# Linear attention block: how x arrives transposed, which queue carries the other loads, and where the q tiles stand

## The chip, the cores and the metric

The kernel runs on one core of a Trainium2 chip. The metric is the time of one execution on the device in microseconds, the median of several runs. "TensorE", "VectorE", "ScalarE", "GpSimd" and "SyncE" appear in the profile as PE (with PEld for its weight loads), DVE, ACT, POOL and SP. "SPq" and "ACTq" are the DMA-issuing instructions of SP and ACT.

## The reference

One linear attention block on x of shape 1 x 2048 x 640 with 32 heads of 20 columns, in bf16:

```python
qkv = x @ wqkv                      # 640 -> 3 * 640, split in q, k, v per head
phi = lambda t: where(t > 0, t + 1, exp(t)) + 1e-6
pq, pk = phi(q), phi(k)
kv  = einsum("bhsd,bhse->bhde", pk, v)      # 20 x 20 per head
z   = einsum("bhsd->bhd", pk)
num = einsum("bhqd,bhde->bhqe", pq, kv)
den = einsum("bhqd,bhd->bhq", pq, z)[..., None] + 1e-6
out = (num / den) @ wo
```

## The kernel before, in words

x is needed in two layouts: as it stands (`xn`, rows on the partitions) and transposed (`xT`, columns on the partitions). Transposed blocks are written by DMA transposes, `load_xT` (line 167): x is cut into five blocks of rows (`XCH`, line 162: 256, 256, 512, 512, 512 rows), and each block into five column tiles of 128, which gives 25 transposes, all issued by SP.

The work has four stages.

1. **k stage**, `k_tile` (line 220), 16 tiles of 128 rows. For each half of the columns TensorE does five matmuls of 128x320 (line 225) with a block of `xT` as weights and `wk` moving; ACT takes the exponential (L235), DVE does the minimum (L237) and the sum that gives `pk` (L240). Eight PSUM banks hold four tiles.
2. **state stage**, `p_step` (line 245): for each half of the columns and each of the 16 row tiles five matmuls (L249) add x-transposed times pk into banks 0 to 4. In each half two q tiles (`q_tile`, line 269: five matmuls of 128x512, then ACT and DVE as in the k stage; L275, L283, L285, L288) stand between the steps and two behind them, in banks 5 to 7. There are 20 q tiles in all. DVE adds up z (L294).
3. **middle**: z is finished (`z_finish`), the state is multiplied with wv (`kv_group`), masked, and multiplied with wo (`w2_group`, six groups). The resulting matrix w2 goes out to DRAM and back in another row order (`w2_rows`: a write of two DMAs, a wait, five reads). The rest of the q tiles, the denominators (`den`: matmuls L391, two ACT operations) and the division (`normalize`, L407) stand between.
4. **output stage**, `out_tile` (line 410), 16 tiles: ten matmuls (L416), copies by ACT and DVE, a DMA out.

Before the k stage TensorE does `warm(n)` matmuls of 128x512 on zeros (L216).

The order on each engine is the order of the calls in the program's text. A small planner (`Plan`, line 18) adds the semaphore waits: an operation waits until the writers of what it reads, and the readers and writers of what it writes, are done; a PSUM bank is such a thing. Each engine runs its list strictly in order, and an engine that issues a DMA (SP, or ACT between its operations) can do nothing else until that issue is through. `w_cols` loads the columns of wqkv; `load_rest` (line 184) issues, all on ACT: `wk` in two halves, `wqn`, the four quarters of `xn`, `wv`, `wog` in two pieces, and then the load of ACT's function table. `permute_wq` (line 205) reorders `wqn` into `wqp` on POOL, which the q tiles read.

Of the kernel before, what the change touches and what calls it, by code (L numbers as in the profile page):

```python
# [82 lines left out]
def bass_standalone__linear_attn_block__prompt_kernel(nc, x, wqkv, wo, out):  # L83
    B, S, D = x.shape
    assert (B, S, D) == (1, 2048, 640)
    H, DH = 32, 20
    NC_ = D // 128
    NT = S // 128
    HALF = D // 2
# [5 lines left out]
    with contextlib.ExitStack() as ctx:  # L95
# [48 lines left out]
        def pool_const():  # L144
            P.add("dve", lambda e: e.memset(zero[:, :], 0.0), writes=["zero"])
            P.add("dve", lambda e: e.memset(ones[:, :], 1.0), writes=["ones"])
            P.add("dve", lambda e: e.memset(eps[:, :], 1e-6), writes=["eps"])  # L147
            P.add("pool", lambda e: e.memset(wv[:, NC_ * D:], 0.0), writes=["wvpad"])
            P.add("pool", lambda e: e.memset(hm[:, :], 1.0), writes=["hm"])
            P.add("pool", lambda e: e.memset(bm[:, :], 1.0), writes=["bm"])  # L150
            for t, w, name in ((hm, 4, "hm"), (bm, DH, "bm")):
                n = t.shape[1] // w
                for lo in (True, False):
                    P.add("pool", lambda e, t=t, w=w, n=n, lo=lo: e.affine_select(
                        out=t[:, :].rearrange("p (a b) -> p a b", b=w),
                        in_=t[:, :].rearrange("p (a b) -> p a b", b=w),
                        pattern=[[-w if lo else w, n], [0, w]],
                        base=0 if lo else w - 1,
                        channel_multiplier=1 if lo else -1,
                        compare_op=ALU.is_ge, fill=0.0), reads=[name], writes=[name])  # L160
# [5 lines left out]

        def load_xT():
            for i, (a, b) in enumerate(XCH):
                for c in range(NC_):
                    P.add("sp", lambda e, a=a, b=b, c=c: e.dma_start(  # L170
                        xT[:, c * S + a:c * S + b], x[0, a:b, 128 * c:128 * c + 128],
                        transpose=True), writes=[("xT", i, c)], dma=True)

        def xT_keys(a, b):
            return [("xT", i, c) for i, (p, q) in enumerate(XCH) if p < b and a < q
                    for c in range(NC_)]

        def w_cols(dst, lo, hi, col, key, eng="act"):
            P.add(eng, lambda e: e.dma_start(
                dst[:, 0:NC_ * D].rearrange("p (c n) -> p c n", n=D)[:, :, lo:hi],  # L180
                wqkv[:, col + lo:col + hi].rearrange("(c p) n -> p c n", p=128)),
                writes=[key], dma=True)

        def load_rest():
            w_cols(wk, 0, HALF, D, ("wk", 0))
            w_cols(wk, HALF, D, D, ("wk", 1))
            w_cols(wqn, 0, D, 0, "wqn")
            for q in range(4):
                P.add("act", lambda e, q=q: e.dma_start(
                    xn[:, 4 * q * D:4 * (q + 1) * D].rearrange("p (t n) -> p t n", n=D),  # L190
                    x[0, 512 * q:512 * (q + 1), :].rearrange("(t p) n -> p t n", p=128)),
                    writes=[("xn", q)], dma=True)
            w_cols(wv, 0, D, 2 * D, "wv")
            P.add("act", lambda e: e.dma_start(
                wog[0:GW, 0:5 * D].rearrange("p (g n) -> p g n", n=D),
                wo[0:5 * GW, :].rearrange("(g p) n -> p g n", p=GW)),
                writes=["wog"], dma=True)
            P.add("act", lambda e: e.dma_start(
                wog[0:gsz[5], 5 * D:6 * D], wo[5 * GW:D, :]), writes=["wog5"], dma=True)
            tl = mybir.InstLoadActFuncSet(  # L200
                name=nc.get_next_instruction_name(),
                act_func_set_id=ACT_TABLE_SET_LN_EXP, ins=[], outs=[])
            P.add("act", lambda e: e.add_instruction(tl), writes=["table"])  # L203

        def permute_wq():

# [7 lines left out]
        def warm(n):  # L214
            for _ in range(n):
                P.add("pe", lambda e: e.matmul(  # L216
                    bank(7), zero[:, 0:128], zero[:, :], start=True, stop=True),
                    reads=["zero"], writes=[("bank", 7)])
# [103 lines left out]
        def z_finish(b):  # L322
            def mm(e):
                for c in range(NC_):
                    r = e.matmul(bank(b, 1, off=c), zs[:, 128 * c:128 * c + 128],
                                 ones[:, 0:1], start=True, stop=True)
                return r
            P.add("pe", mm, reads=["zs", "ones"], writes=[("bank", b)])
            P.add("dve", lambda e: e.tensor_copy(zc[:, 0:NC_], bank(b, NC_)),
                  reads=[("bank", b)], writes=["zc"])  # L330
            for c in range(NC_):
                P.add("dve", lambda e, c=c: e.tensor_scalar(  # L332
                    zb[:, 128 * c:128 * c + 128], hm[:, :], zc[:, c:c + 1], None, ALU.mult),
                    reads=["hm", "zc"], writes=[("zb", c)])
# [27 lines left out]
        def w2_group(g, b):  # L362
            n = gsz[g]
            for h in range(2):
                P.add("pe", lambda e, h=h: e.matmul(
                    bank(b + h, HALF, parts=n), kvt[0:n, GW * g:GW * g + n],
                    wog[0:n, g * D + HALF * h:g * D + HALF * (h + 1)], start=True, stop=True),
                    reads=[("kvt", 0 if g < 4 else g - 3), "wog", "wog5"],
                    writes=[("bank", b + h)])
            P.add("act", lambda e: e.copy(  # L370
                fold(w2g[0:n, g * D:(g + 1) * D]), two_banks(b, parts=n)),
                reads=[("bank", b), ("bank", b + 1)], writes=[("w2g", g)])
# [15 lines left out]
        def den(sbk, b):  # L388
            def mm(e):
                for c in range(NC_):  # L390
                    r = e.matmul(bank(b), zb[:, 128 * c:128 * c + 128],  # L391
                                 pq[:, c * S + BK * sbk:c * S + BK * (sbk + 1)],
                                 start=(c == 0), stop=(c == NC_ - 1))
                return r
            P.add("pe", mm, reads=[("zb", c) for c in range(NC_)]
                  + [("pq", sbk, c) for c in range(NC_)], writes=[("bank", b)])
            i = sbk % 2
            P.add("act", lambda e: e.activation(lb[i][:, :], bank(b), ACTF.Ln, bias=eps[:, 0:1]),  # L398
                  reads=[("bank", b), "eps", "table"], writes=[("lb", i)])
            P.add("act", lambda e: e.activation(rd[i][:, :], lb[i][:, :], ACTF.Exp, scale=-1.0),  # L400
                  reads=[("lb", i)], writes=[("rd", i)])

        def normalize(sbk):
            i = sbk % 2
            for c in range(NC_):
                v = pq[:, c * S + BK * sbk:c * S + BK * (sbk + 1)]
                P.add("dve", lambda e, v=v: e.tensor_tensor(v, v, rd[i][:, :], ALU.mult),  # L407
                      reads=[("rd", i), ("pq", sbk, c)], writes=[("pq", sbk, c)])
# [20 lines left out]
                reads=[("osb", j, 0), ("osb", j, 1)], writes=[("out", st)], dma=True)  # L429


        pool_const()
        load_xT()
        load_rest()
        permute_wq()
        warm(9)
        for st in range(NT):
            k_tile(st)
        zst = z_steps()
# [3 lines left out]
        def next_q(b):  # L443
            q_tile(*qs[qi[0]], b)
            qi[0] += 1

        for h in range(2):
            for st in range(NT):
                p_step(h, st)
                if zst and st % 2 == 1:  # L450
                    zst.pop(0)()
                if st in (5, 11):
                    next_q(5 + qi[0] % 3)
            p_out(h)
            next_q(5 + qi[0] % 3)
            next_q(5 + qi[0] % 3)
        for f in zst:
            f()
        z_finish(4)

        kv_group(0)
        next_q(5)
        next_q(6)
        den(0, 7)
        w2_group(0, 2)
        w2_group(1, 0)
        normalize(0)
        next_q(5)
        w2_group(2, 2)
        w2_group(3, 0)  # L470
        next_q(6)
        den(1, 7)
        w2_group(4, 2)
        w2_group(5, 0)
        w2_rows()
        normalize(1)
        while qi[0] < 15:
            next_q((3, 4, 5, 6)[qi[0] % 4])
        next_q(3)
        next_q(4)  # L480
        den(2, 7)
        next_q(5)
        normalize(2)
        next_q(6)
        next_q(2)
        for st in range(2):
            out_tile(st)
        den(3, 6)
# [56 lines left out]
```

## Time and profile before

| | us |
|---|---|
| median of 3 runs (131.49 to 131.9) | 131.84 |
| the profiled execution | 131.94 |
| its span, first to last instruction | 130.2 |
| TensorE busy (share of the span) | 105.9 (81%) |
| VectorE busy | 66.6 (51%) |
| ScalarE busy | 41.9 (32%) |
| first k matmul starts | 14.92 |
| first state matmul starts | 48.78 |
| first output matmul starts | 103.74 |

All times of the trace count from the start of the span. The profiled execution lies 1.7 us above its span. A row of the timeline gives the start, the time taken, the engine, the line and the operation, merged over equal neighbours, and in brackets the idle time before it with what ended it. In the view of waits, a row reads: who waited, for whom, microseconds in all, how often, the longest. Queue q1 carries what SP issues, q10 what ACT issues; in the views of the DMA, a queue's row gives packets, megabytes and the share of 16 engines.

### The profile page before, as it was taken

The numbers are of one execution on the slowest core, as the hardware profiler recorded it, in microseconds if no ns is written. First come the engines' busy times: TensorE is split into PE (matmuls) and PEld (weight loads), VectorE is DVE, ScalarE is ACT, GpSimd is POOL, SyncE is SP. The second block draws the span as 40 slices with busy tenths as digits, with TensorE's granted clock in tenths as the row PEclk, the third lists the DMA queues.
The fourth block names the chain that finished last, engine by engine and source line by source line (L and its number), as shares of the span: only waits on it lengthen the run. The fifth ranks groups of instructions, "written<-read, shape, count | busy, mean of one in ns | idle before, by whom it ended". The sixth has DMA issues, their size and how long they took to land.

```text
span 130.2 us, 1712 instructions
## 1 busy us (share of the span) xinstructions
PE 105.9 (81%) x655; PEld 65.1 (50%) x661; DVE 66.6 (51%) x132; ACT 41.9 (32%) x73; POOL 5.7 (4%) x16
## 2 busy tenths in 40 slices
PE   6600498309999979999999999989599689999991
PEld 2100254105677757666566668534244256777770
DVE  0000015700488889899923056767586963743431
ACT  0000062301255450101601034288756425323230
POOL 7009000000000000000000000000000000000000
PEclk9999999975799999999999999999999999999999
DMA  3999999994553000000000000000273511243332
GB/s 76 316 249 278 339 321 301 210 198 89 118 58 70 0 0 0 5 0 3 3 0 0 5 0 0 0 0 0 59 196 91 162 44 57 103 151 104 137 114 101
DMA packets 20137, 12.88 MB, mean 99 GB/s; under 512 B 11554, under 2 KB 20130, under 8 KB 20130
## 3 DMA queue, kind: packets, MB, share of 16 engines
q1 hardware_dynamic: 14729, 6.89, 22.4%
q10 hardware_dynamic: 5401, 5.90, 16.1%
q8 instruction: 5, 0.08, 0.3%
q14 instruction: 2, 0.02, 0.0%
HBM read 6.72 MB, written 3.44 MB: 78 GB/s over the span
## 4 chain that ended last, share of the span: by engine, by line
PE 63%; SPq 15%; DVE 6%; ACT 6%; DMA 6%; issue 2%
PE ps L249 17%; PE ps L416 16%; SPq L170 15%; PE ps L225 14%; PE ps L275 13%; DMA xT<-in_x_dram 6%; PE ps L391 3%; DVE pq L288 2%; ACT lb L398 2%; ACT w2g L370 1%; DVE pq L407 1%; ACT rd L400 1%; ACT eq L283 1%; DVE eq L285 1%; DVE zb L332 1%
## 5 line engine op out<-in xcount | busy, mean ns | idle before, releaser
L225 PE MATMUL ps<-wk,xT 128*128 128x320 bf16 x160 | 27.3, 341 | 15.5 <-DMA xT<-in_x_dram 15.0
L225 PEld LDWEIGHTS ps<-wk,xT 128*128 128x128 bf16 x160 | 17.3, 110 | 26.1 <-issue 17.3
L275 PE MATMUL ps<-xT,wqp 128*128 128x512 bf16 x95 | 22.5, 379 | 1.7 <-ACT w2g L370 1.4
L416 PE MATMUL ps<-w2p,pq 128*128 128x320 bf16 x160 | 22.2, 299 | 1.8 <-DMA w2p<-w_rows 1.2
L249 PE MATMUL ps<-pk,xn 128*128 128x320 bf16 x160 | 22.7, 299 | 0.7 <-DVE pk L240 0.7
L283 ACT ACTIVATE eq<-ps 128x512 bf16<-128x512 f32 x20 | 11.9, 597 | 27.2 <-PE ps L275 26.7
L237 DVE TENSOR_SCALAR ek<-ek 128x640 bf16<-128x640 bf16 x16 | 5.2, 327 | 29.9 <-ACT ek L235 29.9
L416 PEld LDWEIGHTS ps<-w2p,pq 128*128 128x128 bf16 x160 | 15.5, 98 | 8.6 <-issue 1.7
L249 PEld LDWEIGHTS ps<-pk,xn 128*128 128x128 bf16 x160 | 15.5, 98 | 8.0 <-DVE pk L240 1.0
L235 ACT ACTIVATE ek<-ps 128x640 bf16<-128x640 f32 x16 | 11.3, 704 | 19.4 <-PE ps L225 19.3
L275 PEld LDWEIGHTS ps<-xT,wqp 128*128 128x128 bf16 x100 | 9.6, 98 | 11.7 <-ACT w2g L370 1.7
L288 DVE SCALAR_TENSOR_TENSOR pq<-ps,eq 128x512 bf16<-128x512 f32 x20 | 13.8, 692 | 0.7
L240 DVE SCALAR_TENSOR_TENSOR pk<-ps,ek 128x640 bf16<-128x640 f32 x16 | 13.2, 825 | 0.5
L425 DVE CAST osb<-ps 128x320 bf16<-128x320 f32 x16 | 7.8, 490 | 10.8 <-PE ps L416 10.8
L285 DVE TENSOR_SCALAR eq<-eq 128x512 bf16<-128x512 bf16 x20 | 5.8, 292 | 13.5 <-ACT eq L283 13.2
L423 ACT CAST osb<-ps 128x320 bf16<-128x320 f32 x16 | 6.8, 425 | 14.7 <-PE ps L416 14.7
L407 DVE TENSOR_TENSOR pq<-pq,rd 128x512 bf16<-128x512 bf16 x20 | 7.1, 420 | 3.8 <-ACT rd L400 3.8
L203 ACT ACT_TABLE_LOAD x1 | 1.3, 1283 | 16.9 <-issue 16.9
L294 DVE TENSOR_TENSOR za<-pk 128x1280 f32<-128x1280 bf16 x4 | 5.8, 1482 | 0.0
L216 PE MATMUL ps<-zero 128*128 128x512 bf16 x9 | 4.0, 631 | 1.3 <-DVE eps L147 1.3
L391 PE MATMUL ps<-pq,zb 128*128 128x512 bf16 x19 | 4.8, 379 | 0.1
L294 DVE TENSOR_TENSOR za<-za 128x1280 f32<-128x1280 f32 x3 | 4.4, 1483 | 0.0
(30 smaller groups left out, 35.0 us busy)
## 6 DMA issues: line engine op xcount, KB each, us to landing
xn<-in_x_dram ACTq DMA_DIRECT2D x4, 640.0 KB, 12.6
out_dram<-osb SPq DMA_DIRECT2D x16, 160.0 KB, 1.8
wk<-in_wqkv_dram ACTq DMA_DIRECT2D x2, 400.0 KB, 4.2
wqn<-in_wqkv_dram ACTq DMA_DIRECT2D x1, 800.0 KB, 8.0
wv<-in_wqkv_dram ACTq DMA_DIRECT2D x1, 800.0 KB, 14.9
w2p<-w_rows SPq DMA_DIRECT2D x5, 160.0 KB, 2.8
wog<-in_wo_dram ACTq DMA_DIRECT2D x1, 750.0 KB, 17.5
w_rows<-w2g SPq DMA_DIRECT2D x1, 750.0 KB, 5.3
```

The costliest lines, as they stand in the source:

```text
L170: P.add("sp", lambda e, a=a, b=b, c=c: e.dma_start(xT[:, c * S + a:c * S + b], x[0, a:b, 128 * c:128 * c + 128], transpose=True), writes=[ ...
L225: r = e.matmul(bank(b + h, HALF), xT[:, c * S + 128 * st:c * S + 128 * st + 128], wk[:, c * D + HALF * h:c * D + HALF * (h + 1)], start=(c ...
L235: P.add("act", lambda e: e.activation(fold(t[:, :]), two_banks(b), ACTF.Exp), reads=banks + ["table"], writes=[("ek", st % 3)])
L240: P.add("dve", lambda e: e.scalar_tensor_tensor(fold(pk[:, st * D:(st + 1) * D]), two_banks(b), 0.0, fold(t[:, :]), ALU.max, ALU.add), rea ...
L249: r = e.matmul(bank(d, HALF), xn[:, st * D + 128 * d:st * D + 128 * d + 128], pk[:, st * D + HALF * h:st * D + HALF * (h + 1)], start=(st ...
L275: r = e.matmul(bank(b), wqp[:, d * D + 128 * c:d * D + 128 * c + 128], xT[:, d * S + BK * sbk:d * S + BK * (sbk + 1)], start=(d == 0), sto ...
L283: P.add("act", lambda e: e.activation(t[:, :], bank(b), ACTF.Exp), reads=[("bank", b), "table"], writes=[("eq", i)])
L288: P.add("dve", lambda e: e.scalar_tensor_tensor(pq[:, c * S + BK * sbk:c * S + BK * (sbk + 1)], bank(b), 0.0, t[:, :], ALU.max, ALU.add), ...
L294: P.add("dve", lambda e: e.tensor_tensor(d_ap, a, b, ALU.add), reads=ra + rb, writes=[dst])
L391: r = e.matmul(bank(b), zb[:, 128 * c:128 * c + 128], pq[:, c * S + BK * sbk:c * S + BK * (sbk + 1)], start=(c == 0), stop=(c == NC_ - 1))
L407: P.add("dve", lambda e, v=v: e.tensor_tensor(v, v, rd[i][:, :], ALU.mult), reads=[("rd", i), ("pq", sbk, c)], writes=[("pq", sbk, c)])
L416: r = e.matmul(bank(b + h, HALF), pq[:, c * S + 128 * st:c * S + 128 * st + 128], w2p[:, c * D + HALF * h:c * D + HALF * (h + 1)], start=( ...
```

## The change

Each block of rows of x is transposed by one DMA transpose over all 640 columns, so that five instructions stand in place of 25, and `xT` has one key per block in place of five. `wk` stays on ACT, with the table load right behind it; `wqn`, `xn`, `wv` and `wog` are issued by SP, behind the five transposes. The warm-up has 16 matmuls in place of 9. In each half of the state stage one q tile is taken out; the middle gets two more, and its order is another: the w2 groups stand singly between q tiles, `z_finish` comes behind the first of them, and the denominators use bank 4 in place of 7.

```diff
         def load_xT():
             for i, (a, b) in enumerate(XCH):
-                for c in range(NC_):
-                    P.add("sp", lambda e, a=a, b=b, c=c: e.dma_start(
-                        xT[:, c * S + a:c * S + b], x[0, a:b, 128 * c:128 * c + 128],
-                        transpose=True), writes=[("xT", i, c)], dma=True)
+                P.add("sp", lambda e, a=a, b=b: e.dma_start_transpose(
+                    xT[:, :].rearrange("p (c s) -> p c s", s=S)[:, :, a:b], x[0, a:b, :]),
+                    writes=[("xT", i)], dma=True)
...
-        def load_rest():
-            w_cols(wk, 0, HALF, D, ("wk", 0))
-            w_cols(wk, HALF, D, D, ("wk", 1))
-            w_cols(wqn, 0, D, 0, "wqn")
...
+        def load_wk():
+            w_cols(wk, 0, HALF, D, ("wk", 0), "act")
+            w_cols(wk, HALF, D, D, ("wk", 1), "act")
...
+        def load_rest():
+            w_cols(wqn, 0, D, 0, "wqn", "sp")
+            for q in range(4):
+                P.add("sp", lambda e, q=q: e.dma_start(
...
+        load_wk()
+        load_xT()
         pool_const()
-        load_xT()
         load_rest()
         permute_wq()
-        warm(9)
+        warm(16)
...
-                if st in (5, 11):
+                if st == 7:
                     next_q(5 + qi[0] % 3)
...
-        z_finish(4)
-
         kv_group(0)
         next_q(5)
+        z_finish(4)
+        w2_group(0, 2)
         next_q(6)
-        den(0, 7)
-        w2_group(0, 2)
         w2_group(1, 0)
+        den(0, 4)
+        next_q(7)
+        w2_group(2, 2)
+        next_q(5)
+        w2_group(3, 0)
         normalize(0)
+        next_q(6)
+        w2_group(4, 2)
+        next_q(7)
+        w2_group(5, 0)
+        den(1, 4)
+        w2_rows()
         next_q(5)
-        w2_group(2, 2)
-        w2_group(3, 0)
         next_q(6)
-        den(1, 7)
-        w2_group(4, 2)
-        w2_group(5, 0)
-        w2_rows()
         normalize(1)
         while qi[0] < 15:
-            next_q((3, 4, 5, 6)[qi[0] % 4])
+            next_q((7, 2, 3, 5, 6)[qi[0] % 5])
+        next_q(0)
+        next_q(1)
+        den(2, 4)
+        next_q(2)
+        normalize(2)
         next_q(3)
-        next_q(4)
-        den(2, 7)
         next_q(5)
-        normalize(2)
-        next_q(6)
-        next_q(2)
         for st in range(2):
             out_tile(st)
```

On SP, at the program's start, before and then with the change (the tile that is written, the DRAM tensor that is read, the shape, the count):

```order
L170 DMA_TRANSPOSE xT<-in_x_dram 128x256 x10
L170 DMA_TRANSPOSE xT<-in_x_dram 128x512 x15
L375 DMA w_rows<-w2g 120x5x640
L379 DMA w_rows<-w2g 40x640
L383 DMA w2p<-w_rows 128x1x640 x5
```

```order
L169 DMA_TRANSPOSE xT<-in_x_dram 128x5x256 x2
L169 DMA_TRANSPOSE xT<-in_x_dram 128x5x512 x3
L177 DMA wqn<-in_wqkv_dram 128x5x640
L193 DMA xn<-in_x_dram 128x4x640 x4
L177 DMA wv<-in_wqkv_dram 128x5x640
L198 DMA wog<-in_wo_dram 120x5x640
L202 DMA wog<-in_wo_dram 40x640
L375 DMA w_rows<-w2g 120x5x640
```

The 25 transposes have become five, and the eight loads that ACT issued now stand between them and the write of w2.

On ACT, at the program's start, the difference between the two (minus is before):

```order
-L179 DMA wk<-in_wqkv_dram 128x5x320 x2
-L179 DMA wqn<-in_wqkv_dram 128x5x640
-L189 DMA xn<-in_x_dram 128x4x640 x4
-L179 DMA wv<-in_wqkv_dram 128x5x640
-L194 DMA wog<-in_wo_dram 120x5x640
-L198 DMA wog<-in_wo_dram 40x640
-L203 ACT_TABLE_LOAD
+L177 DMA wk<-in_wqkv_dram 128x5x320 x2
+L188 ACT_TABLE_LOAD
```

Eight DMA issues have left the place ahead of the table load and the first exponential.

On PE, from the multiplication with wv (L344) to the output (L416), as it stands with the change (L325 is z, L365 w2, L275 a q tile of five matmuls, L391 a denominator):

```order
L344 MATMUL ps<-pt,wv 40x40 x5
L275 MATMUL ps<-xT,wqp 128x512 x5
L325 MATMUL ps<-ones,zs 128x1 x5
L365 MATMUL ps<-wog,kvt 120x320 x2
L275 MATMUL ps<-xT,wqp 128x512 x5
L365 MATMUL ps<-wog,kvt 120x320 x2
L391 MATMUL ps<-pq,zb 128x512 x5
...
L365 MATMUL ps<-wog,kvt 40x320 x2
L391 MATMUL ps<-pq,zb 128x512 x5
L275 MATMUL ps<-xT,wqp 128x512 x25
L391 MATMUL ps<-pq,zb 128x512 x5
L275 MATMUL ps<-xT,wqp 128x512 x15
```

Before, the w2 matmuls stood in runs of four; now each pair has a q tile or a denominator between it and the next. Behind the last pair there are one denominator, five q tiles, one denominator and three q tiles ahead of the output, as there were before without the first denominator.

More of the change, by code (lines that the diff above doesn't have):

```diff
@@ L168, in load_xT, with w_cols @@
             for i, (a, b) in enumerate(XCH):
-                for c in range(NC_):
-                    P.add("sp", lambda e, a=a, b=b, c=c: e.dma_start(
-                        xT[:, c * S + a:c * S + b], x[0, a:b, 128 * c:128 * c + 128],
-                        transpose=True), writes=[("xT", i, c)], dma=True)
+                P.add("sp", lambda e, a=a, b=b: e.dma_start_transpose(
+                    xT[:, :].rearrange("p (c s) -> p c s", s=S)[:, :, a:b], x[0, a:b, :]),
+                    writes=[("xT", i)], dma=True)
         def xT_keys(a, b):
-            return [("xT", i, c) for i, (p, q) in enumerate(XCH) if p < b and a < q
-                    for c in range(NC_)]
-        def w_cols(dst, lo, hi, col, key, eng="act"):
+            return [("xT", i) for i, (p, q) in enumerate(XCH) if p < b and a < q]
+        def w_cols(dst, lo, hi, col, key, eng):
             P.add(eng, lambda e: e.dma_start(
@@ L182, in w_cols @@
                 writes=[key], dma=True)
-        def load_rest():
-            w_cols(wk, 0, HALF, D, ("wk", 0))
-            w_cols(wk, HALF, D, D, ("wk", 1))
-            w_cols(wqn, 0, D, 0, "wqn")
[L188 to L199, printed above, removed]
+        def load_wk():
+            w_cols(wk, 0, HALF, D, ("wk", 0), "act")
+            w_cols(wk, HALF, D, D, ("wk", 1), "act")
             tl = mybir.InstLoadActFuncSet(
@@ L203, in load_rest @@
             P.add("act", lambda e: e.add_instruction(tl), writes=["table"])
+        def load_rest():
+            w_cols(wqn, 0, D, 0, "wqn", "sp")
+            for q in range(4):
+                P.add("sp", lambda e, q=q: e.dma_start(
+                    xn[:, 4 * q * D:4 * (q + 1) * D].rearrange("p (t n) -> p t n", n=D),
+                    x[0, 512 * q:512 * (q + 1), :].rearrange("(t p) n -> p t n", p=128)),
+                    writes=[("xn", q)], dma=True)
+            w_cols(wv, 0, D, 2 * D, "wv", "sp")
+            P.add("sp", lambda e: e.dma_start(
+                wog[0:GW, 0:5 * D].rearrange("p (g n) -> p g n", n=D),
+                wo[0:5 * GW, :].rearrange("(g p) n -> p g n", p=GW)),
+                writes=["wog"], dma=True)
+            P.add("sp", lambda e: e.dma_start(
+                wog[0:gsz[5], 5 * D:6 * D], wo[5 * GW:D, :]), writes=["wog5"], dma=True)
         def permute_wq():
```

## The prediction

> **What bounds the kernel now.** I read the chain that ended last first. By line it says:
>
> ```profile
> PE 63%; SPq 15%; DVE 6%; ACT 6%; DMA 6%; issue 2%
> ```
>
> SPq and DMA, a fifth of the span, are the transposes of x. Next, TensorE's timeline of the k stage, from its start to the first state matmul:
>
> ```profile
> 14.92 5.49 PE L225 MATMUL ps<-wk,xT 128*128 128x320 bf16 x20 [9.64 <-DMA xT<-in_x_dram]
> 20.98 2.88 PE L225 MATMUL ps<-wk,xT 128*128 128x320 bf16 x20 [0.56 <-issue]
> 29.20 18.93 PE L225 MATMUL ps<-wk,xT 128*128 128x320 bf16 x120 [5.34 <-DMA xT<-in_x_dram]
> 48.78 0.45 PE L249 MATMUL ps<-pk,xn 128*128 128x320 bf16 x2 [0.66 <-DVE pk L240]
> 34.79 13.34 PE L225 MATMUL ps<-wk,xT 128*128 128x320 bf16 x97
> ```
>
> TensorE waits for x until 14.92 and again before 29.20. The same 20 matmuls take 5.49 us at 14.92 and 2.88 at 20.98: behind each long wait the clock is low for a while. The last row gives the full pace: (13.34 - 0.30) / 96 = 0.136 us from one matmul to the next, 1.36 us for a tile of ten. At that pace 160 matmuls need 21.8 us; the stage takes 48.78 - 14.92 = 33.9. The windows confirm the clock (columns: PE, PEld, DVE, ACT, POOL, clock, DMA share, GB/s):
>
> ```profile
> 29.10:34.20 5.10, 5.00 (x19) 2.78 (x20) 1.15 (x2) 0.70 (x1) 0.00 (x0) 0.50 0.44 98
> 34.40:48.20 13.80, 13.73 (x102) 9.67 (x99) 10.99 (x20) 7.08 (x11) 0.00 (x0) 1.00 0.25 41
> 27.00:29.00 2.00, 0.00 (x0) 0.00 (x0) 0.00 (x0) 0.00 (x0) 0.00 (x0) 0.61 1.17 229
> ```
>
> Why x is late: pieces of the chain show SP's issue of single transposes. The first three rows are one instruction each (256, 256 and 512 rows); the fourth, behind a full queue, is stretched; the fifth is the landing that TensorE awaits.
>
> ```profile
> 0.81 1.22 SPq L170
> 3.35 1.28 SPq L170
> 13.91 1.26 SPq L170
> 18.44 3.05 SPq L170
> 21.53 7.31 DMA xT<-in_x_dram
> ```
>
> One issue costs 1.22 to 1.28 us, for 256 rows and for 512 alike; 25 of them are 32 us, and backpressure makes it 39. Two limits act at once. The DMA view of 8 to 22 us (ACT's queue q10, SP's q1), and that of 27 to 29 us, when q10 is empty:
>
> ```profile
> q10 hardware_dynamic: 2906, 3.61, 85.0%
> q1 hardware_dynamic: 2831, 0.65, 28.2%
> ```
>
> ```profile
> q1 hardware_dynamic: 1895, 0.46, 117.3%
> ```
>
> Beside the other loads x gets 0.65 MB in 14 us, 46 GB/s; alone, with a backlog, 0.46 MB in 2 us, 229 GB/s (window row above). The packets of the two queues come out one for one, 2906 against 2831. [...]
>
> **The change part by part.** (1) *Start of the k stage.* In before, the first x block waits to 14.92. Now it needs `wk` and one transpose. Both halves of wk are issued from 0.80 on:
>
> ```profile
> 0.80 1.02 ACTq L179 DMA_DIRECT2D wk<-in_wqkv_dram  x2
> 2.42 5.66 ACTq L189 DMA_DIRECT2D xn<-in_x_dram  x4
> 1.26 4.02 PE L216 MATMUL ps<-zero 128*128 128x512 bf16 x9 [1.26 <-DVE eps L147]
> DMA to landing us min/median/max: 3.8/4.2/4.7
> DMA to landing us min/median/max: 2.6/8.0/12.5
> ```
>
> wk (the first landing row) is there by 1.3 + 4.7 = 6.0. If nothing of x had moved until then, block 0, 256 x 640 x 2 bytes = 0.33 MB, takes 1.4 us at 229 GB/s: 7.4, and with some 0.6 from last packet to semaphore 8.0 (an undisturbed transpose, the second landing row, needs 2.6 from issue, 1.3 of it the issue). The warm-up ahead of it in TensorE's list: nine matmuls in 4.02 with a tail of 0.2 is 0.427 each, 16 of them end at 1.26 + 6.83 = 8.1. So the first k matmul comes at 8.1: **-6.8**. The nine all ran at half speed, and full speed came 5 to 6 us after TensorE became busy (14.92 to 20.98, 29.20 to 34.79); 6.8 us of warm-up should cover that. [...]
>
> (2) *The k stage.* x in all is 2048 x 640 x 2 = 2.62 MB, 11.4 us at 229 GB/s: landed by 6.0 + 11.4 + 0.6 = 18. Blocks 1 to 4 land by 9.4, 12.3, 15.1 and 18.0; they are needed for tiles 2, 4, 8 and 12, at 8.1 + 1.36 times the tile: 10.8, 13.5, 19.0, 24.4. TensorE never waits and the clock stays up. The stage and the step to the first state matmul (0.66 idle) take 21.8 + 0.7 + 0.1 = 22.6 in place of 33.9: **-11.3**. State starts at 30.7.
>
> This needs a price that the trace doesn't show: the issue of a transpose of five column tiles. Bounds: 1.24 (a price per instruction) and 5 x 1.24 = 6.2 (per column tile). From the needs above, with 1.4 from issue to landing, block 2 lets 3 issues take 13.5 - 0.8 - 1.4 = 11.3: up to 3.8 us each costs nothing. I take 1.3, since twice the rows cost nothing in the rows above. Halfway, a plain issue of 0.51 (1.02 for two) and five times the rest, 0.51 + 5 x 0.73 = 4.2, loses 1.2. The packets' rate is bounded by 46 and 229 GB/s; nothing shares the engines after wk, so I take 229.
>
> (3) *Loads behind x on SP.*
>
> ```profile
> xn<-in_x_dram ACTq DMA_DIRECT2D x4, 640.0 KB, 12.6
> wqn<-in_wqkv_dram ACTq DMA_DIRECT2D x1, 800.0 KB, 8.0
> 14.00:23.00 9.00, 7.52 (x35) 4.37 (x36) 2.30 (x4) 3.16 (x4) 0.00 (x0) 1.00 1.14 317
> 9.93 3.37 POOL L208 COPY wqp<-wqn 128x640 bf16<-128x640 bf16 x5 [6.82 <-DMA wqn<-in_wqkv_dram]
> ```
>
> After x at 17.4, wqn and xn, 0.82 + 2.62 MB, take 11 us at about 317 GB/s: the first quarter of xn is in by 23, the last by 29, before the state stage begins at 30.7; wqp, 3.4 us of POOL after wqn, is ready near 24 and wanted by a q tile near 36. wv and wog (1.6 MB, 5 us more) are wanted near 59. Cost 0, hidden by the k stage; if x ended only at 30, xn would come at 36 to 42. SP's next DMA that anything waits for is w2's, near 72. The table load, before at 16.88 behind ACT's eight issues, is free to run at 2: nothing, since the first exponential was behind the matmuls.
>
> (4) *q tiles.* Two leave the state stage (five times 0.216 each) and two come to the middle: TensorE runs through both, 0 in sum. What changes are the middle's waits:
>
> ```profile
> PE ps L275 <- ACT w2g L370: 1.4, 1, 1.4
> PE ps L416 <- DMA w2p<-w_rows: 1.2, 1, 1.2
> PE ps L416 <- DVE pq L288: 0.5, 1, 0.5
> PE ps L365 <- ACT w2g L370: 0.4, 1, 0.4
> PE ps L275 <- DVE zb L332: 0.2, 1, 0.2
> ```
>
> The w2 copies now each have a q tile beside them, so 1.4 + 0.4 go. w2's way through DRAM:
>
> ```profile
> 92.59 0.41 SPq L375 DMA_DIRECT2D w_rows<-w2g  x1
> 103.74 1.52 PE L416 MATMUL ps<-w2p,pq 128*128 128x320 bf16 x10 [1.23 <-DMA w2p<-w_rows]
> 92.62 5.57 PE L275 MATMUL ps<-xT,wqp 128*128 128x512 bf16 x24 [1.37 <-ACT w2g L370]
> 94.87 0.69 DVE L288 SCALAR_TENSOR_TENSOR pq<-ps,eq 128x512 bf16<-128x512 f32 x1
> ```
>
> It takes 103.74 - 92.59 = 11.2, plus some 1.2 of copies behind the last w2 matmul, 12.4; TensorE has ten groups of 1.08 there, 10.8, and a new wait: the fifteenth q tile falls on bank 6, as the one ahead of it does (14 mod 5 picks the last of the list). A bank is free again 94.87 + 0.69 - (92.62 + 1.08) = 1.9 after its matmuls. So 12.7: the 1.2 goes, 1.9 comes. The 0.2 and 0.5 stay or move, up to 0.9 more where DVE is behind. -1.4 - 0.4 - 1.2 + 1.9 + 0.6 = **-0.5**, between -2.5 and +2.
>
> The output stage is unchanged. Sum against the profiled 131.94 (0.1 above the median): 131.9 - 6.8 - 11.3 - 0.5 = **113.3**.
>
> **The rivals.** *A: the issue is paid per column tile.* For it: nothing in this trace has such an instruction, and 1.24 us may be mostly one tile's share. Against: 512 rows cost what 256 do. At 6.2 each plus 0.04, block i lands at 0.8 + 6.24(i + 1) + 1.4, the last at 33.4; four tiles, 5.4, and up to 1 of low clock later the stage ends near 39.5 in place of 29.9: 113.3 + 9.6 = 123, range 116 to 124 with prices from 5 on.
>
> *B, slower: merged transposes keep x's slow rate.* If writing five column blocks at once held the queue to the 46 GB/s of 8 to 22 us, x would need 57 us, and the loads, now behind it in the same queue, could not pass: last block at 63, state at 63 + 5.4 + 0.9 = 69, 20 us late; 152. It gets slower once the last block lands after 48.78 - 6.3 = 42.5, below 2.62 / 36 = 72 GB/s. Against: 229 GB/s as soon as q10 was empty.
>
> *C: the loads behind x come late.* If they were as slow beside other traffic as xn was (12.6 to land, one for one with x), a landing near 5 us after the 30.7 at which the first quarter is wanted would shift all behind it: 118. Against: x is finished before.
>
> *D: it does not do what it says*, each merged transpose being carried out as five with today's pace of SP: only the moved loads help. The issue alone then ends at 0.8 + 32 = 33; that is A's time.
>
> **How the numbers follow.** The forecast has 0.70, with its own range 111 to 116.5 (block 0 up to 1.5 late, the middle at its ends). A and D have 0.16, C 0.06, B 0.07 (0.01 of it next to its break-even), and 0.01 is left for an effect too small to see. The range for 8 in 10 takes the forecast's and most of A and C: 111 to 122.5. A change within 0.3%, some 0.4 us, can't be told from none. Faster are the forecast, A, C, D: 0.92; the same 0.02; slower 0.06.
>
> **What would show it.** Five SP transposes of under 4 us each; first L225 near 8.1 and no wait of L225 on xT after it; L225's 160 matmuls at 0.136 with the clock at 1.0; first L249 near 30.7 with no wait on xn; a wait of about 2 us of one L275 on DVE's pq in the middle, none of L416 on w2p. Wrong it is made by issues of over 4 us, by x at under 150 GB/s, or by a low clock when block 0 lands.

## The result, and the profile after

The changed kernel takes 111.85 us (median; 111.82 to 111.9), before it was 131.67 (130.63 to 131.9): a ratio of 0.851, 95% interval 0.846 to 0.856. The forecast was 113.3. The profiled execution takes 111.86 with a span of 110.1.

In the chain that ended last, the 15% that SP's queue held are gone; the 6% of DMA are now a single wait, the one for block 0 of x. TensorE is busy for 92% of the span in place of 81%:

```profile
PE 70%; DVE 15%; DMA 6%; ACT 5%; issue 1%
PE 101.5 (92%) x662; PEld 64.0 (58%) x668; DVE 66.9 (61%) x132; ACT 41.9 (38%) x73; POOL 5.9 (5%) x16
```

TensorE's timeline, from the start to the state stage and then around the middle's one long wait and the first output tiles:

```profile
1.25 5.16 PE L216 MATMUL ps<-zero 128*128 128x512 bf16 x16 [1.25 <-DVE eps L147]
7.49 21.89 PE L225 MATMUL ps<-wk,xT 128*128 128x320 bf16 x160 [1.08 <-DMA xT<-in_x_dram]
30.05 5.61 PE L249 MATMUL ps<-pk,xn 128*128 128x320 bf16 x40 [0.66 <-DVE pk L240]
...
76.08 3.41 PE L275 MATMUL ps<-xT,wqp 128*128 128x512 bf16 x15 [1.75 <-DVE pq L288]
...
83.64 2.20 PE L416 MATMUL ps<-w2p,pq 128*128 128x320 bf16 x15
86.15 0.85 PE L416 MATMUL ps<-w2p,pq 128*128 128x320 bf16 x5 [0.31 <-DVE pq L288]
87.30 1.03 PE L391 MATMUL ps<-pq,zb 128*128 128x512 bf16 x4 [0.30 <-DVE pq L288]
```

The k stage is one row of 160 matmuls in 21.89 us: no wait within it, and full pace from the first. Of SP's side the tile view of xT shows the five issues (shortest, median, longest in ns) and the time from issue to landing. The windows of 7 to 10 and of 7 to 17 us, and the queue row of 7 to 10, show the rate of x with hardly anything else under way:

```profile
L169 SPq DMA_TRANSPOSE xT<-in_x_dram x5: 1343/3055/3314, 0.8 to 11.5; - x5
DMA to landing us min/median/max: 5.3/6.1/6.6
7.00:10.00 3.00, 2.51 (x19) 1.85 (x20) 0.21 (x1) 0.70 (x1) 0.00 (x0) 1.00 1.25 282
7.00:17.00 10.00, 9.51 (x71) 6.88 (x71) 6.15 (x12) 4.23 (x6) 0.00 (x0) 1.00 1.12 223
q1 hardware_dynamic: 3363, 0.84, 124.9%
```

Where the 20.1 us between the two profiled executions come from, all from the start of the span:

| | before | change | difference |
|---|---|---|---|
| start to first k matmul | 14.92 | 7.49 | -7.4 |
| first k to first state matmul | 33.86 | 22.56 | -11.3 |
| first state to first output matmul | 54.96 | 53.59 | -1.4 |
| first output matmul to the end of the span | 26.5 | 26.5 | 0 |

### The profile page after: what moved, and what is told of

Read it like the earlier page. It is cut to its first block, busy times and chain, and to the rows that moved or that the text cites. A ratio compares the mean times of both kernels' runs of the same rounds, so it can differ in the third digit from the quotient of the medians.

```text
span 110.1 us, 1693 instructions
## 1 busy us (share of the span) xinstructions
PE 101.5 (92%) x662; PEld 64.0 (58%) x668; DVE 66.9 (61%) x132; ACT 41.9 (38%) x73; POOL 5.9 (5%) x16
## 4 chain that ended last, share of the span: by engine, by line
PE 70%; DVE 15%; DMA 6%; ACT 5%; issue 1%
PE ps L225 19%; PE ps L416 17%; PE ps L249 15%; PE ps L275 12%; DMA xT<-in_x_dram 6%; DVE pq L288 4%; PE ps L391 4%; DVE za L294 4%; ACT eq L283 2%; DVE eq L285 2%; DVE pq L407 2%; PE ps L344 1%; ACT lb L398 1%; PE ps L365 1%; ACT rd L400 1%
## 5 line engine op out<-in xcount | busy, mean ns | idle before, releaser
L275 PE MATMUL ps<-xT,wqp 128*128 128x512 bf16 x95 | 23.0, 379 | 2.0 <-DVE pq L288 1.8
L249 PE MATMUL ps<-pk,xn 128*128 128x320 bf16 x160 | 22.4, 299 | 0.8 <-DVE pk L240 0.7
L225 PE MATMUL ps<-wk,xT 128*128 128x320 bf16 x160 | 21.9, 299 | 1.1 <-DMA xT<-in_x_dram 1.1
L416 PE MATMUL ps<-w2p,pq 128*128 128x320 bf16 x160 | 22.2, 299 | 0.3 <-DVE pq L288 0.3
L249 PEld LDWEIGHTS ps<-pk,xn 128*128 128x128 bf16 x160 | 15.5, 98 | 7.9 <-DVE pk L240 1.0
L225 PEld LDWEIGHTS ps<-wk,xT 128*128 128x128 bf16 x160 | 15.6, 98 | 7.5 <-issue 1.5
L416 PEld LDWEIGHTS ps<-w2p,pq 128*128 128x128 bf16 x160 | 15.6, 98 | 7.0 <-DVE pq L288 0.6
L235 ACT ACTIVATE ek<-ps 128x640 bf16<-128x640 f32 x16 | 11.3, 704 | 15.7 <-PE ps L225 15.7
L275 PEld LDWEIGHTS ps<-xT,wqp 128*128 128x128 bf16 x100 | 9.6, 98 | 12.2 <-DVE pq L288 2.2
L237 DVE TENSOR_SCALAR ek<-ek 128x640 bf16<-128x640 bf16 x16 | 6.1, 380 | 10.5 <-ACT ek L235 10.4
L216 PE MATMUL ps<-zero 128*128 128x512 bf16 x16 | 5.2, 494 | 1.3 <-DVE eps L147 1.3
L261 ACT CAST pt<-ps 128x320 bf16<-128x320 f32 x6 | 2.2, 434 | 9.7 <-PE ps L249 9.7
L391 PE MATMUL ps<-pq,zb 128*128 128x512 bf16 x19 | 4.8, 380 | 0.4 <-DVE pq L288 0.3
L208 POOL COPY wqp<-wqn 128x640 bf16<-128x640 bf16 x5 | 3.6, 756 | 16.9 <-DMA wqn<-in_wqkv_dram 16.9
## 6 DMA issues: line engine op xcount, KB each, us to landing
wv<-in_wqkv_dram SPq DMA_DIRECT2D x1, 800.0 KB, 14.3
```

The source lines that it names most:

```text
L225: r = e.matmul(bank(b + h, HALF), xT[:, c * S + 128 * st:c * S + 128 * st + 128], wk[:, c * D + HALF * h:c * D + HALF * (h + 1)], start=(c ...
L235: P.add("act", lambda e: e.activation(fold(t[:, :]), two_banks(b), ACTF.Exp), reads=banks + ["table"], writes=[("ek", st % 3)])
L249: r = e.matmul(bank(d, HALF), xn[:, st * D + 128 * d:st * D + 128 * d + 128], pk[:, st * D + HALF * h:st * D + HALF * (h + 1)], start=(st ...
L275: r = e.matmul(bank(b), wqp[:, d * D + 128 * c:d * D + 128 * c + 128], xT[:, d * S + BK * sbk:d * S + BK * (sbk + 1)], start=(d == 0), sto ...
L391: r = e.matmul(bank(b), zb[:, 128 * c:128 * c + 128], pq[:, c * S + BK * sbk:c * S + BK * (sbk + 1)], start=(c == 0), stop=(c == NC_ - 1))
L416: r = e.matmul(bank(b + h, HALF), pq[:, c * S + 128 * st:c * S + 128 * st + 128], w2p[:, c * D + HALF * h:c * D + HALF * (h + 1)], start=( ...
```

## The experiments

All of them are edits of the changed kernel, and are compared with its 111.85; it gave 111.94 when run again beside the last two. The kernel before gave 131.1 beside the first four.

**The loads back on ACT, the five transposes kept.** Two reasons for the late x had been given, the 25 issues and the sharing of the DMA engines. This and the next run undo one edit each.

```diff
-            w_cols(wqn, 0, D, 0, "wqn", "sp")
+            w_cols(wqn, 0, D, 0, "wqn", "act")
...
-                P.add("sp", lambda e, q=q: e.dma_start(
+                P.add("act", lambda e, q=q: e.dma_start(
```

(the same for wv and both pieces of wog; the table load comes behind them)

> The changed kernel with wqn, xn, wv and wog issued by ACT again, behind wk and ahead of the table load; the five merged transposes stay. If the sharing of the DMA engines held x back (packets of the two queues alternate one for one), x moves at about 200 packets a microsecond until ACT's 5.9 MB are out near 26 us: block 2 lands near 22, block 4 near 30, TensorE waits for x in the k stage, first state matmul near 41, time 121 to 125. If the number of issues alone held x back, x is in by 18 as with the change; only the table load comes late, behind ACT's issues near 17, which holds the first exponential: first state matmul near 36, time 116 to 118, and no wait of the k matmuls on x after the first.

Measured: 127.65 us (127.5 to 128.75). TensorE's k stage, and the queues from 8 to 20 us:

```profile
7.62 2.93 PE L227 MATMUL ps<-wk,xT 128*128 128x320 bf16 x20 [0.72 <-DMA xT<-in_x_dram]
13.64 2.89 PE L227 MATMUL ps<-wk,xT 128*128 128x320 bf16 x20 [3.08 <-DMA xT<-in_x_dram]
27.05 19.23 PE L227 MATMUL ps<-wk,xT 128*128 128x320 bf16 x120 [10.52 <-DMA xT<-in_x_dram]
```

```profile
q10 hardware_dynamic: 2919, 3.63, 83.0%
q1 hardware_dynamic: 2916, 0.74, 27.6%
```

With only five issues x is still held back for 14.3 us in three waits. 2919 packets of ACT's queue went out in these 12 us against 2916 of SP's, one for one; but a packet of x is 256 bytes and one of the loads 1280, so that x gets a sixth of the bytes, 0.74 MB in 12 us, 62 GB/s. The sharing alone does it. The table load, which stands behind ACT's issues again (the last of them ends at 16.78, it starts at 16.81), held the exponentials only to 18.2, long before block 2 landed, so it decides nothing here. The sum was 3 to 7 us short: block 2 came at 27.0 where 22 was expected, since x had about 240 packets a microsecond to 20 us and only about 170 from 21 to 25; why it got fewer there stays open. The clock is at half from 19.0 to 32.7, which costs some 2.8 more behind the 10.5 us wait (19.23 for 120 matmuls that take 16.4 at full pace), as it did in the kernel before.

**25 transposes again, the loads behind them on SP.**

```diff
-                P.add("sp", lambda e, a=a, b=b: e.dma_start_transpose(
-                    xT[:, :].rearrange("p (c s) -> p c s", s=S)[:, :, a:b], x[0, a:b, :]),
-                    writes=[("xT", i)], dma=True)
+                for c in range(NC_):
+                    P.add("sp", lambda e, a=a, b=b, c=c: e.dma_start(
+                        xT[:, c * S + a:c * S + b], x[0, a:b, 128 * c:128 * c + 128],
+                        transpose=True), writes=[("xT", i, c)], dma=True)
```

(and with it five keys of `xT` per block in place of one)

> The changed kernel with 25 transposes in place of five; the loads stay behind them on SP. If the issue of a transpose costs 1.26 us whatever the queue, block i lands at 0.8 + 6.4 (i + 1) + 1.4: 8.6, 15, 21.5, 28, 34; TensorE waits for each, the clock drops in between, first state matmul near 40.5, time 121 to 123. If the sharing of the engines alone held x back, x is in near 18 as with the change and the time stays at 111.9.

Measured: 124.15 us (123.79 to 124.48). SP's issues, and TensorE's waits:

```profile
0.81 33.40 SPq L170 DMA_TRANSPOSE xT<-in_x_dram  x25
L170 SPq DMA_TRANSPOSE xT<-in_x_dram x25: 1214/1261/2340, 0.8 to 32.9; - x25
```

```profile
PE ps L227 <- DMA xT<-in_x_dram: 9.1, 5, 3.3
42.62 5.61 PE L251 MATMUL ps<-pk,xn 128*128 128x320 bf16 x40 [1.02 <-DVE pk L242]
```

With no other load beside x once wk is in, an issue still takes 1.26 us, and 25 of them 33.4: now the issue alone decides, some 2 us later at the state stage than the 40.5 expected (stretches of half clock stand at 15.0 to 18.4 and 21.8 to 25.2). So each of the two limits alone keeps x late. What each edit is worth by itself can be estimated by adding the middle's 1.4 us (below) back: the merging alone takes the 131.1 that the kernel before gave in the same rounds to about 129.0, the moving alone to 125.5, both to 113.2, all three with 16 warm-ups. That is -2 and -6 apart, -18 together.

**What an issue costs.** In the change the first issue took 1.34 us and the other four 2.8 to 3.3. Blocks of 256 rows, then of 128 rows:

```diff
-        XCH = [(0, 256), (256, 512), (512, 1024), (1024, 1536), (1536, 2048)]
+        XCH = [(256 * i, 256 * i + 256) for i in range(8)]
```

```diff
-        XCH = [(0, 256), (256, 512), (512, 1024), (1024, 1536), (1536, 2048)]
+        XCH = [(128 * i, 128 * i + 128) for i in range(16)]
```

> The changed kernel with eight blocks of 256 rows, so eight transposes of 5 x 256. In the changed kernel the first issue took 1.34 us, the four after it 2.8 to 3.3. If the price of an issue is 1.3 and the rest is a full queue (data at 1130 packets a microsecond), the eight take 11 to 14 us together, 1.3 to 1.8 each, and the time stays within 0.5 of 111.9. If about 3 us is the price of an instruction over five column tiles, the eight take 24 us, block 7 lands at 26.5, one wait of 1 to 2 us appears late in the k stage and the time is 113 to 114.

> The changed kernel with sixteen blocks of 128 rows. With a price of 1.3 per issue the sixteen take 22 us, tile k lands at 0.8 + 1.38 (k + 1) + 1.4, always ahead of TensorE's 1.36 a tile from 7.5 on: time 111.5 to 112.3. With 3 us per issue they take 50 us, TensorE waits for every tile, first state matmul near 53, time 135. If each issue costs 0.5 plus something per column tile and per 16 rows, the sixteen come in between.

Measured: 111.87 us (111.83 to 111.92) and 112.14 (111.75 to 112.58). The tile view of xT, of the first and then of the second:

```profile
L169 SPq DMA_TRANSPOSE xT<-in_x_dram x8: 1346/1755/3011, 0.8 to 14.2; - x8
```

```profile
L169 SPq DMA_TRANSPOSE xT<-in_x_dram x16: 1255/1278/1968, 0.8 to 21.4; - x16
```

The eight issues took 15.1 us together, a little over the 11 to 14 expected. The sixteen have a median of 1.278 us: an instruction over five column tiles costs what one over a single tile costs (1.261 in the run before), and what half the rows cost. No run has a transpose of 512 rows over five tiles with an empty queue, but two rows speak for a full queue as the cause of the 3 us in the change. Its 2560 packets of 256 bytes take 2.9 us at the 223 GB/s of 7 to 17 us; and with the loads on ACT, where x moved at 62 GB/s (10.6 us for the same packets), the longest of the same five issues took 11.1 us:

```profile
L169 SPq DMA_TRANSPOSE xT<-in_x_dram x5: 1342/3198/11102, 0.8 to 27.2; - x5
```

The time doesn't move, since x is ahead of TensorE in all three cuts, but for the wait on block 0.

**Nine warm-up matmuls.**

```diff
-        warm(16)
+        warm(9)
```

> The changed kernel with nine warm-up matmuls in place of 16. In the changed kernel the ninth matmul came at full pace, with the clock up at 4.4 us. If the clock rises after about 3.2 us of work, nine matmuls (to 5.3) are enough to raise it and the 2.1 us of idle time up to the first k matmul at 7.4 don't lower it: 111.9. If, as the prediction had it, 5 to 6 us of work are needed, the first k matmuls run at half speed for 1 to 3 us: first state matmul 0.7 to 2.5 later, 112.6 to 114.4.

Measured: 113.57 us in the median, but the six executions lie between 111.61 and 114.6. The profiled one took 113.52. Its windows (the last columns are clock, DMA share, GB/s) and its timeline:

```profile
8.00:11.40 3.40, 3.40 (x15) 1.97 (x13) 0.78 (x2) 0.70 (x1) 0.00 (x0) 0.50 1.09 234
11.50:20.00 8.50, 8.50 (x64) 6.13 (x63) 6.41 (x13) 4.23 (x6) 0.00 (x0) 1.00 1.01 237
```

```profile
1.26 3.75 PE L216 MATMUL ps<-zero 128*128 128x512 bf16 x9 [1.26 <-DVE eps L147]
7.47 23.58 PE L225 MATMUL ps<-wk,xT 128*128 128x320 bf16 x160 [2.46 <-DMA xT<-in_x_dram]
```

Neither expectation holds as written. Nine matmuls do raise the clock (the record of the trace has it up at 4.6), but with 2.46 us without work up to the first k matmul it is down again from 8.0 to 11.4, and the k stage takes 23.58 in place of 21.89. In one execution of six nothing was lost (111.61).

Two other traces have longer stretches of half clock: 6.8 us, from 27.4 to 34.3, in the kernel before, and 13.6, from 19.0 to 32.7, with the loads on ACT. Both began within a wait of TensorE on x, of 5.34 us up to 29.20 and of 10.52 up to 27.05. Their windows, taken just inside the ends, give a clock of 0.50 throughout:

```profile
27.50:34.20 6.70, 5.00 (x19) 2.78 (x20) 1.15 (x2) 0.70 (x1) 0.00 (x0) 0.50 0.62 131
19.10:32.60 13.50, 5.55 (x21) 3.15 (x22) 5.31 (x10) 2.40 (x5) 0.00 (x0) 0.50 1.10 223
```

The length of the idle time does not decide alone. The 2.46 us here, behind nine matmuls, were followed by half clock, and the 3.08 ahead of block 1 with the loads on ACT were not: 20 matmuls took 2.89 us there, at a clock of 1.00 from 13.6 to 16.6. In the change 1.08 us behind 16 matmuls left the clock at 1.00 from 7.4 to 29.4. What decides is not shown by these traces, nor is what makes the spread of the other five executions, since they left none. The 16 are worth 1.7 us in the median, and a steadier time.

**The old order of the state stage and the middle.** The edit puts back the minus lines of that part of the change's diff.

> The changed kernel with the state stage and the middle in the old order (two q tiles within each half, w2 groups in runs of four, denominators in bank 7). If the old waits return (1.4 and 0.4 on w2's copies, 1.2 on w2's way through DRAM, 0.2) and the 1.75 on bank 6 goes, the time is 113.0 to 113.5, 1.4 more than the change. If the order is worth nothing by itself, 111.9.

Measured: 113.22 us (113.0 to 113.3). TensorE's waits:

```profile
PE ps L275 <- ACT w2g L370: 1.4, 1, 1.4
PE ps L416 <- DMA w2p<-w_rows: 1.0, 1, 1.0
PE ps L416 <- DVE pq L288: 0.8, 1, 0.8
PE ps L365 <- ACT w2g L370: 0.4, 1, 0.4
PE ps L275 <- DVE zb L332: 0.2, 1, 0.2
```

The old waits are back, 3.8 us of them against 2.4 in the change: the new order is worth 1.4 us.

**The wait on bank 6.** The fifteenth q tile goes to bank 7:

```diff
-            next_q((7, 2, 3, 5, 6)[qi[0] % 5])
+            next_q(7)
```

> The changed kernel with the fifteenth q tile in bank 7 in place of bank 6, which the fourteenth has just filled. If the 1.75 us wait of TensorE is lost time, the output stage begins 1.6 earlier, w2 having landed at 81.5 against the 81.9 at which it would then be read: 110.2 to 110.7. If the middle is bound by DVE, behind whose list the later q tiles and denominators then wait, the wait moves to L391 or L416 and the time is 111.4 to 111.9.

Measured: 111.24 us (111.09 to 111.31). The wait of TensorE, and what stands ahead of it on DVE:

```profile
PE ps L391 <- DVE pq L288: 1.4, 2, 1.1
75.98 1.76 DVE L407 TENSOR_TENSOR pq<-pq,rd 128x512 bf16<-128x512 bf16 x5
77.97 0.69 DVE L288 SCALAR_TENSOR_TENSOR pq<-ps,eq 128x512 bf16<-128x512 f32 x1
78.72 1.25 PE L391 MATMUL ps<-pq,zb 128*128 128x512 bf16 x5 [1.11 <-DVE pq L288]
```

Only 0.6 of 1.75 comes out; the wait has moved to the denominators. The time lies between the two expectations. What is late is DVE: its five divisions of block 1 take 1.76 us just ahead of the fifteenth q tile's two operations, which the denominator of block 2 needs. So the divisions were moved:

```diff
         next_q(6)
-        normalize(1)
         while qi[0] < 15:
             next_q(7)
+        normalize(1)
         next_q(0)
         next_q(1)
         den(2, 4)
         next_q(2)
-        normalize(2)
         next_q(3)
         next_q(5)
+        normalize(2)
```

> The fifteenth q tile in bank 7, and the divisions of blocks 1 and 2 put behind the q tiles that stood behind them (normalize(1) behind the fifteenth, normalize(2) behind the last q tile). If the middle's waits of TensorE come from the 1.76 us of five divisions on DVE ahead of a q tile's two operations, they all go: 1.75 + 0.3 + 0.3 less than the change, 109.3 to 109.8, with w2's landing near 81.5 as the next bound. If DVE is short of time there in any order, the wait moves to the divisions' readers and the time stays at 111.2.

Measured: 109.21 us (109.12 to 109.45). That is just below the 109.3 to 109.8 of the first expectation. All waits of TensorE that are left:

```profile
PE ps L216 <- DVE eps L147: 1.3, 1, 1.3
PE ps L225 <- DMA xT<-in_x_dram: 1.1, 1, 1.1
PE ps L249 <- DVE pk L240: 0.7, 1, 0.7
```

The middle has none any more; the first output matmul comes at 81.94 in place of 83.64, though the state stage began 0.2 later than in the change. DVE had the time; the order on it was at fault. The run doesn't say which of the two moved groups is worth how much.

**A better kernel.** Last, the first block of x in two, on top of that:

```diff
-        XCH = [(0, 256), (256, 512), (512, 1024), (1024, 1536), (1536, 2048)]
+        XCH = [(0, 128), (128, 256), (256, 512), (512, 1024), (1024, 1536), (1536, 2048)]
```

> The same, with the first block of 256 rows of x cut in two of 128. If the first k matmul waits for block 0's last packet, it comes 0.3 to 0.5 earlier: 109.0 to 109.4. If wk's second half or the warm-up is there no earlier, nothing: as the one before within 0.2.

Measured: 108.82 us (108.67 to 109.19), the ratio to the kernel before 0.832 (0.828 to 0.835), where the change in the same rounds has 0.855 (0.852 to 0.858).

```profile
6.89 21.91 PE L225 MATMUL ps<-wk,xT 128*128 128x320 bf16 x160
29.46 5.61 PE L249 MATMUL ps<-pk,xn 128*128 128x320 bf16 x40 [0.66 <-DVE pk L240]
```

The k stage begins at 6.89, with no wait on x; it now follows the warm-up directly. The gain of 0.4 us is as expected for block 0; the time itself lies 0.2 below the range.

## Why the prediction was right, point by point

- *Start of the k stage, -6.8; measured -7.4.* The warm-up and block 0 were both put too late. The warm-up was costed at 0.427 us throughout, on the reading that full speed needs 5 to 6 us of work: 16 were to end at 8.1. In this execution the clock is up at 4.4, 3.2 us after the work began, and the last of the 16 was issued at 6.0. But that isn't a fixed time either: when the same kernel was run again, the clock came up at 7.2 and the 16 took 6.55 us, near the 6.83 of the sum:

```profile
1.26 6.55 PE L216 MATMUL ps<-zero 128*128 128x512 bf16 x16 [1.26 <-DVE eps L147]
```

  The k stage followed them there at 7.64, without a wait on x. From the start of the work to the full clock it was 3.2 us here and 5.9 there, and 5.7 and 5.1 behind the two waits of the kernel before; the 16 took 5.16 to 6.55 us in the ten traces that have them. So the reading of 5 to 6 us fits that execution and not this one; what sets the time is not shown. That the stage began at nearly the same time in both is luck: here it waited for block 0, there for the warm-up. (The windows print a clock of 1.00 up to the first recorded change; that it is low there shows in the pace, 0.43 us for a matmul in place of 0.215.) Block 0 landed at 7.4, not 8.0, and wk's second half at 7.3, not 6.0: x and wk moved at the same time (from 2 to 6 us x's queue carried 0.33 MB and wk's 0.69), so x did not stand still until wk was in. The stage waited 1.08 for x.
- *k stage, -11.3; measured -11.3.* 22.56 against 22.6. No wait, no low clock, as put. x was in by 16.8 (the last issue at 11.5 and 5.3 more) in place of 18. The 0.6 from the last packet to the semaphore, in this sum and in that of block 0, was the author's estimate; here the last packet of x ended at 16.4, 0.4 before that landing. Its rate was not the reason: the 282 GB/s of 7 to 10 us did not last, and the mean of 7 to 17 us is 223, near the 229 of the sum. x had a start instead, since it moved beside wk: 0.66 MB had gone by 7.6 us, where the sum had nothing before 6.0 and so 0.37 by then.
- *Issue price, taken as 1.3 between 1.24 and 6.2.* The first one took 1.34, and sixteen in a row a median of 1.28 (the run with 128 rows). The bound of the sum by which up to 3.8 us cost nothing also held: the 2.8 to 3.3 of the other four cost nothing.
- *Loads behind x, 0; measured 0.* No L249 and no q tile waits for a load. The timeline of SP and the view of xn:

```profile
15.40 3.37 SPq L193 DMA_DIRECT2D xn<-in_x_dram  x4
DMA to landing us min/median/max: 7.8/9.7/11.1
```

  The last of the four is issued at 17.6 and in by 28.7, before 30.05.
- *Middle, -0.5; measured -1.4.* The waits on w2's copies and on w2's way through DRAM are gone, and the wait on bank 6 is there with 1.75 (1.9 was predicted). The mis-sized term is the +0.6 for waits that "stay or move", on top of the old ones: up to the first output matmul 1.75 stands in place of 0.2 + 0.4 + 1.4 + 1.2 = 3.2, which is the whole -1.4, and behind it 0.31 and 0.30 stand in place of the old 0.5. What the prediction had too simple is the 1.75 itself: with another bank only 0.6 came out, as DVE was late there too.
- *The rivals.* A and D fall with the issues, 1.28 for an instruction over five tiles; their time is nevertheless what the run with 25 transposes gave (124.15 against 123). B falls with the 223 GB/s, yet its premise, x at 46 GB/s beside other loads, is what the run with the loads on ACT shows, 62 GB/s; only the merging has no part in it. C falls, as x and xn were in early.

The sum, 113.3, was 1.4 too high: 0.6 at the start, 0.9 in the middle, and 0.1 of rounding back.

## What to carry to other kernels

Two limits on the same stream hide each other: here the issue (256 or 512 packets per 1.26 us) and the packets of two queues that went out one for one (2831 of x against 2906 in 8 to 22 us of the kernel before, about 200 a microsecond) were both at work; removing one alone was worth some 2 or 6 us, and removing both 18. Before counting on an edit that removes a limit, work out the rate that the next one allows. Loads that aren't needed yet belong behind the urgent ones in the same queue: here x had 46 and 62 GB/s beside them, one packet of 256 bytes against one of 1280, and 223 ahead of them. And when a stage is bound by several engines in turn, look at what stands just ahead of the awaited operation on its engine: two groups of five divisions that nothing needed yet cost 2 us.

## What the runs showed of the hardware that was not expected

- An issue of a DMA transpose on SP took 1.26 to 1.28 us with room in the queue, for 512 rows by one column tile as for 128 rows by five.
- Merged or not, the transposes move at the same pace while they move: 282 GB/s in 7 to 10 us of the change, and about 290 in the steady parts of 27 to 29 us of the kernel before (40 slices of 0.05 us):

```profile
GB/s 31 41 62 257 169 292 287 287 297 282 292 287 186 57 292 266 307 266 317 266 307 276 237 103 231 297 276 297 282 292 287 287 257 83 98 128 179 215 230 246
```

  The 229 that the prediction took is the mean over this stretch with its gaps, as 223 is over 7 to 17 us of the change. Where the gaps come from stays open.
- With the same 16 warm-up matmuls the clock of TensorE came up 3.2 us after the first of them in the change and 5.9 us after it when the same kernel was run again. Stretches of half clock lasted 3.4 us (the run with nine), 6.8 (the kernel before) and 13.6 (the loads on ACT), and an idle time of 2.46 us was followed by one where another of 3.08 was not.
